# Order of work in one attention step, and fp16 parts of the attention output made on GpSimd

## The chip, the cores and the metric

The kernel runs on one NeuronCore of a Trainium2 chip. The metric is the device time of one execution in microseconds (us). Three runs of the kernel before gave a median of 3019.1 us (3017.41 to 3022.62).

## The reference

One transformer block on a [1, 2048, 576] fp32 input: LayerNorm, attention with 32 heads of 18 columns each, a residual; LayerNorm, a gated MLP of width 4608, a residual.

```python
qkv = (x @ wqkv).reshape(B, S, 3, 32, 18)            # q, k, v
scores = einsum("bhqd,bhkd->bhqk", q, k) * 18 ** -0.5
o = einsum("bhqk,bhkd->bhqd", softmax(scores), v)
h = x + o.reshape(B, S, 576) @ wo                    # x inside attention is layernorm(x)
out = h + (gelu(g @ w_gate) * (g @ w_up)) @ w_down   # g = layernorm(h)
```

## The kernel before

Matrices are held as fp16 pairs (a rounded part and the rest) so that fp16 products come out near fp32. The span has three stages: the q, k, v products (to about 230 us), attention (to about 1690 us), and the MLP.

**Attention** works on groups of four heads (`g`, 8 of them) and blocks of 512 queries (`qc`, 4 of them): 32 blocks, counted by `n`. One block takes 16 steps (`kt`), each with 128 keys. One step does three things for different blocks at once:

- **scores** (`scores_pair`, L453 to L463): for two heads at a time TensorE multiplies K by Q into a two-bank PSUM tile (`pair0`, `pair1` in turn), and ScalarE takes the exponential of both banks in one instruction (L463) into one of four buffers `pes`.
- **maxima** (`max_unit`, L408 to L425): softmax needs the row maximum beforehand, so the same products with queries on the partitions are computed once more, 28 units of 128 queries by 512 keys ahead. One call gives a pair: two matmuls (L420) into two banks of a ring of three (`m_ring`), each followed by a VectorE reduction over 512 columns (L423). A bank is written again three products later, after its reduction. `max_finish` (L427 to L446) folds a block's maxima: three small VectorE instructions (L430, L432, L433), then, a few steps later, a TensorE transpose into a ring bank (L438), a VectorE copy (L440) and eight small DMAs on SyncE's queue.
- **weighing** (`weigh`, L465 to L469): four matmuls (L467; eight records in the profile) add the previous step's exponentials times V into bank 3. It works one step behind the scores.

At a block's end `out_block` (L471) copies the sum to SBUF on ScalarE (L476), transposes it in a ring bank (four matmuls, L480), and on VectorE takes the reciprocal (L483) and multiplies (L485) into `o`, a [128, 4, 72] fp32 tile with two buffers. Then `o` is split into fp16 parts in `nat16`: a cast (L490) and one or two subtractions (L491, and L493 where the columns pass 512). In the last head group SyncE's transposing DMAs (L226) read these parts, and `wo_block` multiplies them by `wo` (as `fill`, a generator that is drawn between the scores, from step 4 of a block on).

**What sets the order.** TensorE's instructions are issued in the order in which the program is written (a manual schedule), by the loop over `n` and `kt` in the diff below. On VectorE, ScalarE and GpSimd a planner sets each queue's order at build time by its own estimates of when operands are ready; each queue is then strictly in order. GpSimd's queue also issues half of the loads of the next group's stacked q and k rows (L407, L408, 12 per group); SyncE's issues the other half.

Of the kernel before, what the change touches and what calls it, by code (L numbers as in the profile page):

```python
# [17 lines left out]
D = 576  # L18
H = 32
DH = 18  # L20
# [9 lines left out]
def tile_block(  # L30
# [17 lines left out]
    nc = tc.nc  # L48
# [4 lines left out]
    NT = S // P  # L53
# [161 lines left out]
    LM = D + TAIL  # L215
# [9 lines left out]
    def turn(rows, t):  # L225
        nc.sync.dma_start_transpose(XT[:, :, t * P : (t + 1) * P], rows)  # L226
# [42 lines left out]
    def run(it):  # L269
        for _ in it:  # L270
            pass
# [8 lines left out]
    def take(it, n=1):  # L280
        for _ in range(n):
            next(it, None)
# [105 lines left out]
    def init_set(st):  # L388
        for pr in range(2):
            for j in range(2):  # L390
                nc.sync.dma_start(
                    st[pr][1][64 * j + R1 : 64 * j + R1 + 2].rearrange("p (a b) -> p a b", b=256),
                    neg.unsqueeze(1).to_broadcast([2, S // 256, 256]))

    def load_stacks(g):
        st = sets[g % 2]
        for pr in range(2):
            eng = nc.sync if pr == 0 else nc.gpsimd
            Q, K = st[pr]
            for j in range(2):  # L400
                h = 4 * g + 2 * pr + j
                o = 64 * j
                kr = slice(D + h * DH, D + (h + 1) * DH)
                qr = slice(h * DH, (h + 1) * DH)
                for i, (qs, ks) in enumerate(((qk_hi, qk_hi), (qk_hi, qk_lo), (qk_lo, qk_hi))):
                    rows = slice(o + i * DH, o + (i + 1) * DH)
                    eng.dma_start(Q[rows], qs[qr])  # L407
                    eng.dma_start(K[rows], ks[kr])  # L408
# [45 lines left out]
    def scores_pair(n, kt, pr):  # L454

        g, qc = divmod(n, NB)
        pS = next(pair_ring)
        Q, K = sets[g % 2][pr]
        for j in range(2):
            r = half(j, R1 + 2)  # L460
            nc.tensor.matmul(pS[:, j, :TB], K[r, kt * P : (kt + 1) * P],  # L461
                             Q[r, qc * TB : (qc + 1) * TB], start=True, stop=True)
        nc.scalar.activation(pes[(2 * kt + pr) % NPE], pS[:, :, :TB], AF.Exp, scale=ex_sc)  # L463

    def weigh(n, kt, acc):  # L465
        for hh in range(4):
            nc.tensor.matmul(acc[32 * hh : 32 * hh + 32, :TB],  # L467
                             Vg[n // NB][:, kt * G4 + hh * VC : kt * G4 + hh * VC + 32],
                             pes[(2 * kt + hh // 2) % NPE][:, hh % 2],  # L469
                             start=(kt == 0), stop=(kt == NT - 1))  # L470

    def out_block(n, acc):

        g, qc = divmod(n, NB)
        oT = oTs[n % 2]
        nc.scalar.copy(oT, acc[:, :TB])  # L476
        yield
        pt = next(m_ring)
        for i in range(TPB):
            nc.tensor.transpose(pt[:, i * P : (i + 1) * P], oT[:, i * P : (i + 1) * P], id32)  # L480
        v = pt[:, :TB].rearrange("p (t h c) -> p t h c", h=4, c=32)
        rc = small.tile([P, TPB, 4, 1], F32, tag="rc", name="rc")
        nc.vector.reciprocal(rc, v[:, :, :, DH : DH + 1])  # L483
        o = small.tile([P, TPB, 4 * DH], F32, tag="o", name="o")
        nc.vector.tensor_mul(o.rearrange("p t (h c) -> p t h c", c=DH), v[:, :, :, :DH],  # L485
                             rc.to_broadcast([P, TPB, 4, DH]))
        f0 = g * 4 * DH
        f1 = min(f0 + 4 * DH, NK * P)
        dst = nat16[:, qc * TPB : (qc + 1) * TPB]
        nc.scalar.copy(dst[:, :, f0 : f0 + 4 * DH], o)  # L490
        nc.vector.tensor_sub(dst[:, :, LM + f0 : LM + f1], o[:, :, : f1 - f0], dst[:, :, f0:f1])  # L491
        if f1 < f0 + 4 * DH:
            nc.vector.tensor_sub(dst[:, :, D:LM], o[:, :, f1 - f0 :], dst[:, :, f1:D])  # L493

    NS = NG * NB
    UPS = TPB * NB
# [3 lines left out]
    def maxima():  # L500

        late = None
        for n in range(NS):
            mx = small.tile([P, TPB, 4, NB], F32, tag="mx", name="mx")
            for u in range(UPS):
                for i, _ in enumerate(max_unit(n, u, mx)):
                    yield
                    if late is not None and 2 * u + i == LAG:
                        for _ in late:
                            pass  # L510
                        late = None
            late = max_finish(n, mx)
            next(late)
        for _ in late:
            pass
# [22 lines left out]
    def wo_block(b):  # L538

        for t in range(b * TPB, (b + 1) * TPB):  # L540
            for i in range(2):
                ws = slice(i * HALF, (i + 1) * HALF)
                xb = xbs[(2 * t + i) % 3]
                nc.sync.dma_start(xb, xv[:, t, ws])
                pt = next(m_ring)
                run(accumulate(pt[:, :HALF], products(slice(t * P, (t + 1) * P), oh, ol, ws)))
                nc.vector.scalar_tensor_tensor(nat[:, t, ws], pt[:, :HALF], u_o, xb,
                                               op0=ALU.mult, op1=ALU.add)
                yield
            row_stats(nat[:, t], t)  # L550
        rstd_of(b * TPB, TPB)
        for t in range(b * TPB, (b + 1) * TPB):
            normed(y, nat[:, t], t)
            split_rows(ys[t % 2], y, nc.vector.tensor_copy if b < NB - 1 else nc.scalar.copy)
            turn(ys[t % 2], t)
            yield
# [84 lines left out]
    def qk_block(b):  # L641
        for j in (0, 4, 5):
            yield from qk_tile(j, b, next(m_ring))

    def v_block(b):
        for t in range(b * TPB, (b + 1) * TPB):
            yield from v_rows(t)

    def other_products():
        for b in range(1, NB):  # L650
            yield from v_block(b)
        for j in (1, 6, 2, 7, 3, 8):
            for b in range(NB):
                yield from qk_tile(j, b, next(pair_ring)[:, 0])
# [3 lines left out]
    def keep(it):  # L658
        kept.append((yield from it))

    mxs = maxima()
    with tc.manual_schedule(engines={EngineType.PE}):
        for b in range(NB):
            run(qk_block(b))
            if b == min(1, NB - 1):
                run(v_block(0))
        init_set(sets[0])
        load_stacks(0)
        fill = other_products()
        side = iter(())  # L670
        take(fill, 14)
        for i in range(2 * AHEAD):
            take(mxs)
            take(fill, 2 - i % 2)
        prev = None
        for n in range(NS):
            g, qc = divmod(n, NB)
            acc = singles[3]
            for kt in range(NT):
                for pr in range(2):  # L680
                    scores_pair(n, kt, pr)
                    take(mxs, UPS // NT)
                    if g < NG - 1 or kt >= NT // 4:
                        take(fill)
                    take(side)
                if prev is not None:
                    weigh(*prev)
                    if prev[0] != n:
                        ob = out_block(prev[0], prev[2])
                        next(ob)  # L690
                prev = (n, kt, acc)
                if n and kt == 1:
                    take(ob)
                    if n > NS - NB:
                        for t in range((qc - 1) * TPB, qc * TPB):
                            turn(nat16[:, t], t)
                        run(fill)
                        fill = wo_block(qc - 1)
                if g == 0 and qc == 0 and kt == NT - 1:
                    run(fill)  # L700
                    init_set(sets[1])
                if g + 1 < NG and kt == 2 and qc == (1 if g == 0 and NB > 1 else 0):
                    load_stacks(g + 1)
                if n == min(2, NS - 2) and kt == 2:
                    side = prepare_wo()
                if n == NS - NB and kt == 2:
                    load_gate_up(0)
                if n == max(NS - 2, NS - NB) and kt == NT * 3 // 4:
                    run(side)
                    side = keep(split_gate_up(0))  # L710
        weigh(*prev)
        for _ in out_block(prev[0], prev[2]):
            pass
        run(side)
        run(fill)
# [45 lines left out]
```

## Time and profile before

| | |
|---|---|
| median of 3 runs | 3019.1 us |
| the profiled execution's own time | 3017.52 us |
| its span | 3015.8 us |
| busy: TensorE / VectorE / ScalarE / GpSimd | 2792.8 / 1993.3 / 1454.6 / 62.9 us |
| granted TensorE clock, mean | 0.995 |
| maxima reductions (L423) | 2048, 1283.2 us busy |
| exponentials (L463) | 1024, 1088.0 us busy |
| casts of `o` on ScalarE (L490) | 32, 13.5 us busy |
| subtractions of `o` on VectorE (L491, L493) | 32 and 4, 13.3 and 1.7 us busy |

A row of a timeline gives the start in us from the span's beginning, the duration (from the first start to the last end where several instructions are merged, with their count behind an x), the engine, the source line, output and inputs; brackets hold the idle time ahead and what ended it. In the names, `pair` and `bank` are PSUM tiles, `A` and `W` are the two regions that hold the stacked q and k rows in turn, `WK` holds the exponentials.

### The profile page before, as it was taken

Reading aid. Unit: us, or ns where it says so; the run is one execution under the profiler, and the core shown is the slowest. Engines: PE = TensorE matmul, PEld = TensorE weight load, DVE = VectorE, ACT = ScalarE, POOL = GpSimd, SP = SyncE. Lnnn points to the kernel's source line nnn. Section 1 sums busy time; section 2 is a strip of 40 time slices with the busy share of each in tenths; the row PEclk is TensorE's granted clock in tenths of the full one; section 3 lists DMA queues with packets and bytes.
Section 4 is the critical chain, followed back from the end, with each engine's and each line's share of the span. In section 5 each row is a group of like instructions: output and inputs, shape, how many; then the busy total and the mean of one; then the engine's idle time right before and its main releaser. Section 6 shows DMA issues by size and latency. Waiting matters only on the chain.

```text
span 3015.8 us, 42951 instructions
## 1 busy us (share of the span) xinstructions
PE 2792.8 (93%) x17312; PEld 1154.9 (38%) x17312; DVE 1993.3 (66%) x3711; ACT 1454.6 (48%) x1716; POOL 62.9 (2%) x137
## 2 busy tenths in 40 slices
PE   6998888888888888888889999999999999999999
PEld 3531112212111211211123455555555555555555
DVE  7569999999999999999996653443435252524222
ACT  5227777777777777777757422121212121212111
POOL 0000000000000000000000000000000000000000
PEclk9999999999999999999999999999999999999999
DMA  8121000000100000000023420110101010100001
GB/s 222 49 87 32 1 25 1 25 1 1 25 1 25 1 24 2 1 24 5 29 48 87 100 67 7 45 33 19 51 1 52 1 51 1 51 1 1 1 16 48
DMA packets 105433, 95.14 MB, mean 32 GB/s; under 512 B 65872, under 2 KB 79312, under 8 KB 105232
## 3 DMA queue, kind: packets, MB, share of 16 engines
q1 hardware_dynamic: 100256, 83.81, 9.8%
q0 software_dynamic: 4976, 8.56, 1.1%
q8 instruction: 136, 2.23, 0.3%
q14 instruction: 65, 0.53, 0.1%
HBM read 63.70 MB, written 14.16 MB: 26 GB/s over the span
## 4 chain that ended last, share of the span: by engine, by line
PE 74%; DVE 18%; ACT 4%; issue 2%; DMA 2%; SPq 0%; DVEq 0%; ACTq 0%
PE pair L267 30%; PE bank L267 16%; DVE mx L423 15%; PE bank L467 14%; PE bank L420 9%; PE pair L461 4%; ACT WK L463 1%; ACT W L238 1%; ACT V L238 1%; PE bank L480 1%; DVE o L485 0%; ACT V L598 0%; DVE nat L491 0%; DMA A<-qk_hi 0%; DMA WK<-in_A_wqkv_dram 0%
## 5 line engine op out<-in xcount | busy, mean ns | idle before, releaser
L423 DVE TENSOR_REDUCE mx<-bank 128x1 f32<-128x512 f32 x2048 | 1283.2, 682 | 138.4 <-PE bank L420 137.4
L463 ACT ACTIVATE WK<-pair,p_ex_sc 128x1024 f32<-128x1024 f32 x1024 | 1088.0, 1112 | 335.1 <-PE pair L461 333.4
L467 PE MATMUL bank<-WK,V 128*32 128x512 f32 x4096 | 551.9, 610 | 0.1
L267 PE MATMUL pair<-X,V 128*128 128x512 f16 x2240 | 489.0, 379 | 3.1 <-ACT ga L613 3.1
L267 PE MATMUL pair<-X,W 128*128 128x512 f16 x2128 | 469.0, 379 | 1.5 <-ACT ga L613 1.5
L615 DVE SCALAR_TENSOR_TENSOR ga<-pair,p_hsc,ga 128x512 f32<-128x512 f32 x144 | 107.7, 748 | 502.4 <-PE pair L267 502.4
L420 PE MATMUL bank<-W 54*128 54x512 f16 x1024 | 291.5, 378 | 93.2 <-DVE mx L423 91.1
L267 PEld LDWEIGHTS <-WK 128*128 128x128 f16 x3456 | 338.2, 98 | 93.2
L420 PE MATMUL bank<-A 54*128 54x512 f16 x1024 | 283.0, 380 | 80.5 <-DVE mx L423 77.7
L613 ACT ACTIVATE ga<-pair,p_gsc 128x512 f32<-128x512 f32 x144 | 98.8, 686 | 490.2 <-PE pair L267 490.2
L267 PEld LDWEIGHTS <-W 128*128 128x128 f16 x2296 | 222.2, 98 | 273.1 <-issue 16.9
L267 PEld LDWEIGHTS <-V 128*128 128x128 f16 x2240 | 218.7, 98 | 261.6 <-issue 3.9
L616 ACT CAST WK<-ga 128x512 f16<-128x512 f32 x144 | 88.9, 618 | 442.9 <-DVE ga L615 442.9
L634 DVE SCALAR_TENSOR_TENSOR nat<-bank,p_dsc,nat 128x288 f32<-128x288 f32 x288 | 147.9, 515 | 194.9 <-PE bank L267 194.9
L467 PEld LDWEIGHTS bank<-WK,V 128*32 128x32 f32 x4096 | 81.3, 108 | 504.5 <-issue 469.0
L267 PE MATMUL bank<-V,WK 128*128 128x288 f16 x1920 | 239.0, 286 | 0.0
L461 PE MATMUL pair<-W 56*128 56x512 f16 x1024 | 199.1, 384 | 5.8 <-ACT WK L463 5.6
L461 PE MATMUL pair<-A 56*128 56x512 f16 x1024 | 199.9, 385 | 0.3 <-DVE qk L322 0.2
L267 PE MATMUL bank<-W,WK 128*128 128x288 f16 x1536 | 191.4, 286 | 0.0
L617 DVE TENSOR_TENSOR WK<-ga,WK 128x512 f16<-128x512 f32 x144 | 99.3, 690 | 76.3 <-ACT WK L616 76.1
L461 PEld LDWEIGHTS <-W 56*128 56x128 f16 x1024 | 50.2, 94 | 247.9 <-issue 221.0
L461 PEld LDWEIGHTS <-A 56*128 56x128 f16 x1024 | 50.5, 95 | 241.3 <-issue 211.0
(154 smaller groups left out, 1122.0 us busy)
## 6 DMA issues: line engine op xcount, KB each, us to landing
V<-in_B_w_down_dram SPq DMA_DIRECT2D x9, 1152.0 KB
A<-in_B_w_gate_dram SPq DMA_DIRECT2D x9, 1024.0 KB
A<-in_B_w_up_dram SPq DMA_DIRECT2D x9, 1024.0 KB
qk_hi<-qk SPq DMA_DIRECT2D x36, 128.0 KB
qk_lo<-qk SPq DMA_DIRECT2D x36, 128.0 KB
A<-in_A_x_dram SPq DMA_DIRECT2D x32, 144.0 KB
out_dram<-nat SPq DMA_DIRECT2D x16, 288.0 KB
WK<-in_A_wqkv_dram SPq DMA_DIRECT2D x3, 1152.0 KB
```

The costliest lines, as they stand in the source:

```text
L238: nc.scalar.activation(wh[:, c], wf[:, c], AF.Copy, scale=sc)
L267: nc.tensor.matmul(dst, a, b, start=(i == 0), stop=(i == len(pairs) - 1))
L420: nc.tensor.matmul(pms[j][:, :TB], Q[r, q0 : q0 + P], K[r, kc * TB : (kc + 1) * TB], start=True, stop=True)
L423: nc.vector.tensor_reduce(mx[:, t, 2 * pr + j, kc : kc + 1], pms[j][:, :TB], axis=AX.X, op=ALU.max)
L461: nc.tensor.matmul(pS[:, j, :TB], K[r, kt * P : (kt + 1) * P], Q[r, qc * TB : (qc + 1) * TB], start=True, stop=True)
L463: nc.scalar.activation(pes[(2 * kt + pr) % NPE], pS[:, :, :TB], AF.Exp, scale=ex_sc)
L467: nc.tensor.matmul(acc[32 * hh : 32 * hh + 32, :TB], Vg[n // NB][:, kt * G4 + hh * VC : kt * G4 + hh * VC + 32], pes[(2 * kt + hh // 2) % ...
L613: nc.scalar.activation(ga, pg[:, :TB], AF.Gelu_apprx_tanh, scale=gsc)
L615: nc.vector.scalar_tensor_tensor(ga, pu[:, :TB], hsc, ga, op0=ALU.mult, op1=ALU.mult)
L616: nc.scalar.copy(hh[:, f], ga)
L617: nc.vector.tensor_sub(hl[:, f], ga, hh[:, f])
L634: nc.vector.scalar_tensor_tensor(nat[:, t, ws], pt[:, :HALF], dsc, nat[:, t, ws], op0=ALU.mult, op1=ALU.add)
```

## The change

Two edits. In a step, both pairs of maxima used to follow the scores, one after each pair of heads (`take(mxs, UPS // NT)` takes one pair, since `UPS // NT` is 1). Now one pair stands ahead of the scores of all four heads and one behind them, ahead of the weighing. And the split of `o` (L490 to L493) moves to GpSimd: the cast from ScalarE, the subtractions from VectorE.

```diff
         dst = nat16[:, qc * TPB : (qc + 1) * TPB]
-        nc.scalar.copy(dst[:, :, f0 : f0 + 4 * DH], o)
-        nc.vector.tensor_sub(dst[:, :, LM + f0 : LM + f1], o[:, :, : f1 - f0], dst[:, :, f0:f1])
+        nc.gpsimd.tensor_copy(dst[:, :, f0 : f0 + 4 * DH], o)
+        nc.gpsimd.tensor_sub(dst[:, :, LM + f0 : LM + f1], o[:, :, : f1 - f0], dst[:, :, f0:f1])
         if f1 < f0 + 4 * DH:
-            nc.vector.tensor_sub(dst[:, :, D:LM], o[:, :, f1 - f0 :], dst[:, :, f1:D])
+            nc.gpsimd.tensor_sub(dst[:, :, D:LM], o[:, :, f1 - f0 :], dst[:, :, f1:D])
...
             for kt in range(NT):
+                take(mxs)
                 for pr in range(2):
                     scores_pair(n, kt, pr)
-                    take(mxs, UPS // NT)
                     if g < NG - 1 or kt >= NT // 4:
                         take(fill)
                     take(side)
+                take(mxs)
                 if prev is not None:
                     weigh(*prev)
```

On TensorE, in an ordinary step, from one weighing (L467) to the second scores of the next step. Banks 68 to 70 are the ring of the maxima, 66 and 67 the two score tiles, 71 the sum. Before:

```order
L467 MATMUL bank_71<-WK,V 32x512 x4
L461 LDWEIGHTS W
L461 MATMUL pair_66<-W 128x512 [waits Activation_49]
L461 LDWEIGHTS W
L461 MATMUL pair_66<-W 128x512
L420 LDWEIGHTS W
L420 MATMUL bank_69<-W 128x512 [waits DVE_49]
L420 LDWEIGHTS W
L420 MATMUL bank_70<-W 128x512 [waits DVE_49]
L461 LDWEIGHTS W
L461 MATMUL pair_67<-W 128x512 [waits Activation_49]
```

With the change:

```order
L467 MATMUL bank_71<-WK,V 32x512 x4
L420 LDWEIGHTS W
L420 MATMUL bank_69<-W 128x512 [waits DVE_49]
L420 LDWEIGHTS W
L420 MATMUL bank_70<-W 128x512 [waits DVE_49]
L461 LDWEIGHTS W
L461 MATMUL pair_66<-W 128x512 [waits Activation_49]
L461 LDWEIGHTS W
L461 MATMUL pair_66<-W 128x512
L461 LDWEIGHTS W
L461 MATMUL pair_67<-W 128x512 [waits Activation_49]
```

The first maxima now come straight behind the weighing, with two score matmuls fewer between; the two pairs of scores follow each other directly.

On VectorE, at a block's end, where the transposed sum stands in bank 70. Before:

```order
L423 TENSOR_REDUCE mx<-bank_69 128x1 [waits PE_49]
L483 RECIPROCAL rc<-bank_70 128x16 [waits PE_49]
L485 TENSOR_TENSOR o<-bank_70,rc 128x288 [waits DVE_49]
L423 TENSOR_REDUCE mx<-bank_68 128x1 [waits PE_49]
L423 TENSOR_REDUCE mx<-bank_69 128x1 [waits PE_49]
L491 TENSOR_TENSOR nat<-o,nat 128x4x72 [waits Activation_49]
L423 TENSOR_REDUCE mx<-bank_70 128x1 [waits PE_49]
```

With the change:

```order
L423 TENSOR_REDUCE mx<-bank_69 128x1 [waits PE_49]
L483 RECIPROCAL rc<-bank_70 128x16 [waits PE_49]
L423 TENSOR_REDUCE mx<-bank_68 128x1 [waits PE_49]
L485 TENSOR_TENSOR o<-bank_70,rc 128x288 [waits DVE_49,Pool_49]
L423 TENSOR_REDUCE mx<-bank_69 128x1 [waits PE_49]
L423 TENSOR_REDUCE mx<-bank_70 128x1 [waits PE_49]
```

The subtraction has left, one reduction has moved between the reciprocal and the product, and the product now waits for GpSimd, which reads the buffer of two blocks ago.

On GpSimd, where a new group's rows are loaded (`A` here), the queue with the change:

```order
L490 CAST nat<-o 128x4x72 [waits DVE_49]
L407 DMA A<-qk_hi 18x2048 [waits DMASW1_49,PE_49]
L491 TENSOR_TENSOR nat<-o,nat 128x4x72 [waits Pool_49]
L408 DMA A<-qk_hi 18x2048 [waits DMASW2_49]
L407 DMA A<-qk_hi 18x2048 [waits DMASW3_49]
```

Before, only the loads stood there; now the cast and the subtraction stand among them once per group, and alone in the queue for the other blocks.

## The prediction

> **What bounds the kernel now.** I read the page's chain first, then the long middle stage by windows, then the timeline of one step, then the steps that differ from it.
>
> ```profile
> PE 74%; DVE 18%; ACT 4%; issue 2%; DMA 2%; SPq 0%; DVEq 0%; ACTq 0%
> PE pair L267 30%; PE bank L267 16%; DVE mx L423 15%; PE bank L467 14%; PE bank L420 9%; PE pair L461 4%; ACT WK L463 1%; ACT W L238 1%; ACT V L238 1%; PE bank L480 1%; DVE o L485 0%; ACT V L598 0%; DVE nat L491 0%; DMA A<-qk_hi 0%; DMA WK<-in_A_wqkv_dram 0%
> ```
>
> The attention part of the chain is not one engine's: reductions (L423), weighing (L467), maxima products (L420) and, with 4%, scores (L461) alternate. So no engine is full there, and the windows say the same:
>
> ```profile
> 502.25:1523.00 1020.75, 890.97 (x5989) 201.96 (x5987) 944.04 (x1640) 796.28 (x780) 30.65 (x62) 1.00 0.05 12
> ```
>
> In order: length, busy TensorE, weight loads, VectorE (944 of 1021 us, 92%), ScalarE, GpSimd, clock 1.00. One ordinary step shows what closes the loop:
>
> ```profile
> 802.25 0.39 PE L461 MATMUL pair<-W 56*128 56x512 f16 x2
> ...
> 802.48 0.38 PE L420 MATMUL bank<-W 54*128 54x512 f16 x2
> ...
> 802.70 0.38 PE L461 MATMUL pair<-W 56*128 56x512 f16 x2
> ...
> 802.74 2.12 ACT L463 ACTIVATE WK<-pair,p_ex_sc 128x1024 f32<-128x1024 f32 x2 [0.57 <-PE pair L461]
> 802.89 2.48 DVE L423 TENSOR_REDUCE mx<-bank 128x1 f32<-128x512 f32 x4 [0.21 <-PE bank L420]
> ...
> 803.64 0.37 PE L420 MATMUL bank<-W 54*128 54x512 f16 x1 [0.34 <-DVE mx L423]
> ...
> 803.94 1.07 PE L467 MATMUL bank<-WK,V 128*32 128x512 f32 x8
> ...
> 804.94 0.39 PE L461 MATMUL pair<-W 56*128 56x512 f16 x2
> ...
> 805.16 0.38 PE L420 MATMUL bank<-W 54*128 54x512 f16 x2
> ...
> 805.58 2.48 DVE L423 TENSOR_REDUCE mx<-bank 128x1 f32<-128x512 f32 x4 [0.20 <-PE bank L420]
> ```
>
> The step's first reduction starts at 802.89. The fourth maxima product writes the same bank, and starts 0.75 later (803.64). The weighing follows 0.30 after it, TensorE's next matmul 1.00 after that (804.94, the scores), the next first maximum 0.22 behind those (805.16), and its reduction 0.42 later (805.58). 0.75 + 0.30 + 1.00 + 0.22 + 0.42 = 2.69 us, the whole period: each link is on the loop. VectorE's four reductions take 2.48, and stand 0.20 idle. A reduction lasts 0.68 but the next starts 0.60 after it ((2.48 - 0.68) / 3), so VectorE alone could do a step in 4 x 0.60 = 2.40.
>
> **The order inside the step.** The scores' 0.22 leaves the loop, since the first maxima now stand straight behind the weighing. What the head of the queue costs is seen only for scores: from 802.25 to the exponential at 802.74 is 0.49, against 0.42 from a maxima product to its reduction. Part of that 0.07 is ScalarE's answer and part the second matmul it needs; so 0.42 to 0.49 are the ends, and I take 0.43, nearest to the row of the same two engines. The step becomes 0.75 + 0.30 + 1.00 + 0.43 = 2.48 us, 0.21 less, and VectorE's idle time falls from 0.20 to 0.08.
>
> Three other waits must stay covered; let the first maximum start at 0. *Banks:* the second product of the next step writes the bank of the third reduction, which starts 1.20 after the first, lasts 0.68, and is answered 0.07 later (0.75 - 0.68): 1.95 after the first reduction; TensorE comes out of the weighing at 0.75 + 0.30 + 1.00 = 2.05. Cover 0.10. *Exponentials:* the scores start at 0.22, the exponentials 0.49 later at 0.71, and end at 2.83, which is 0.35 into the next step; the second scores, due at 0.44 there, need the tile of the second one. Cover 0.09; and behind them the second maxima wait until 0.43 + 0.75 = 1.18 anyway, though they could go at 0.66, so another 0.52 stands behind it. *Weighing* uses exponentials of the step before, ready at 0.35, and starts at 1.48.
>
> **A block of 16 steps.** The sum's copy (L476) marks blocks:
>
> ```profile
> 502.25 0.58 ACT L476 COPY WK<-bank 128x512 f32<-128x512 f32 x1 [0.18 <-PE bank L467]
> 546.62 0.58 ACT L476 COPY WK<-bank 128x512 f32<-128x512 f32 x1 [0.18 <-PE bank L467]
> ...
> 1525.73 0.58 ACT L476 COPY WK<-bank 128x512 f32<-128x512 f32 x1 [0.18 <-PE bank L467]
> ...
> L476 ACT COPY WK<-bank x32: 585/585/595, 275.1 to 1685.9; 128x512 f32<-128x512 f32 x32
> ```
>
> One block is 44.37 us; from 275.1 to 1525.73 there are 28. Sixteen steps are 43.04; three steps are longer.
>
> *Transposing the maxima.*
>
> ```profile
> 827.86 1.29 DVE L423 TENSOR_REDUCE mx<-bank 128x1 f32<-128x512 f32 x2 [0.20 <-PE bank L420]
> ...
> 828.60 0.37 PE L420 MATMUL bank<-W 54*128 54x512 f16 x1 [0.40 <-DVE mx L423]
> ...
> 829.06 0.20 DVE L440 COPY mT<-bank 32x128 f16<-32x128 f16 x1
> ...
> 829.20 0.37 PE L420 MATMUL bank<-W 54*128 54x512 f16 x1 [0.23 <-DVE mx L423]
> ...
> 831.14 2.48 DVE L423 TENSOR_REDUCE mx<-bank 128x1 f32<-128x512 f32 x4 [0.68 <-PE bank L420]
> ```
>
> The transpose takes a ring bank, so the step's last product waits for the second reduction instead of the first: 831.14 - 827.86 = 3.28, or 0.59 over. The transpose still stands ahead of the second maxima pair and still takes their bank: 0.59 stays.
>
> *Folding the maxima* puts three small instructions between reductions:
>
> ```profile
> 822.48 0.69 DVE L423 TENSOR_REDUCE mx<-bank 128x1 f32<-128x512 f32 x1 [0.20 <-PE bank L420]
> ...
> 823.21 0.68 DVE L423 TENSOR_REDUCE mx<-bank 128x1 f32<-128x512 f32 x1
> ...
> 823.89 0.68 DVE L423 TENSOR_REDUCE mx<-bank 128x1 f32<-128x512 f32 x1
> ...
> 824.57 3.08 DVE L423 TENSOR_REDUCE mx<-bank 128x1 f32<-128x512 f32 x5
> ```
>
> Starts are 0.73, 0.68, 0.68 apart, not 0.60: 0.29 more, which idle time hid (the next first reduction at 824.57 + 0.60 = 825.17, so the step stayed 2.69). Now VectorE needs 2.40 + 0.29 = 2.69 against 2.48: 0.21 over.
>
> *The block's output:*
>
> ```profile
> 858.01 2.48 DVE L423 TENSOR_REDUCE mx<-bank 128x1 f32<-128x512 f32 x4 [0.21 <-PE bank L420]
> ...
> 860.06 0.66 PE L480 MATMUL bank<-id,WK 128*128 128x128 f32 x4
> ...
> 860.64 0.10 PEld L461 LDWEIGHTS <-W 56*128 56x128 f16 x2 [0.17 <-issue]
> ...
> 860.75 0.26 DVE L483 RECIPROCAL rc<-bank 128x16 f32<-128x16 f32 x1 [0.26 <-PE bank L480]
> ...
> 861.04 0.46 DVE L485 TENSOR_TENSOR o<-bank,rc 128x288 f32<-128x288 f32 x1
> ...
> 861.42 1.28 DVE L423 TENSOR_REDUCE mx<-bank 128x1 f32<-128x512 f32 x2
> ...
> 862.98 3.67 DVE L423 TENSOR_REDUCE mx<-bank 128x1 f32<-128x512 f32 x6
> ```
>
> Before: the first reduction comes 3.41 after the last one (861.42 - 858.01), 0.72 over; the third starts at 862.98 instead of 862.62, since the subtraction takes 0.36, and the next first one at 862.98 + 2 x 0.60 = 864.18, 2.76 later, 0.07 over. Together 0.79. So the subtraction cost 0.07 of its 0.36; most of it lay in VectorE's idle time.
> Now: the transposes push the first maxima back by 0.58 (860.06 to 860.64). The reciprocal is done by then (transposes + 0.69 + 0.29 = 0.98, reduction at 0.58 + 0.43 = 1.01). The third and fourth products write the bank out of which `o` is made, so they wait for one reduction and then the product, 0.38 longer (861.04 to 861.42). Together 0.96. Without the second edit the subtraction's 0.36 would come on top where VectorE has 0.08 left, some 0.3 per block, 9 us in all: that is what the move to GpSimd is worth. The cast on ScalarE cost nothing that ends last.
>
> New block: 16 x 2.48 + 0.59 + 0.21 + 0.96 = 41.44; the same sum for before, 43.04 + 0.59 + 0.79 = 44.42, is close to the 44.37 seen. Saved: 44.37 - 41.44 = 2.93; 28 blocks: 82 us.
>
> **Outside these blocks.** 484 steps hold maxima (1024 pairs less 56 taken ahead, two a step); 448 are counted. Of the other 36 about half run with other products drawn in, where TensorE is full; the rest gives 18 x 0.21 = 4 us (466 steps in all). Against it, 20 VectorE instructions of preparing `wo` (five maxima, five splits) and the first gate and up weights (ten maxima) lay partly in the idle time, which shrinks by 0.12 a step: 20 x 0.12 = 2.5 us lost.
>
> **The cost on GpSimd.** No row shows arithmetic like it. Nearest:
>
> ```profile
> masks.py:199 POOL TENSOR_SCALAR_AFFINE_SELECT id<-id 128x128 f32<-128x128 f32 x1 | 0.3, 282 | 0.0
> ```
>
> 0.282 us for 128 columns, so at most 0.63 for the cast's 288 and, with two inputs, 1.27 for the subtraction, 1.9 in all; at least what the two engines take now. `o` has two buffers, so a block (41 us) covers this 20 times, also behind twelve loads. It shows only where a transposing DMA waits for it:
>
> ```profile
> 1688.04 0.43 ACT L490 CAST nat<-o 128x288 f16<-128x288 f32 x1 [1.59 <-DVE o L485]
> ...
> 1688.61 0.42 DVE L493 TENSOR_TENSOR nat<-o,nat 128x256 f16<-128x256 f32 x1
> ...
> 1689.10 6.01 SPq L226 DMA_TRANSPOSE X<-nat  x4
> ```
>
> Now 1.06 from cast to DMA; with GpSimd 1.06 to 1.9. At most twice on the path (here and one block earlier): 0 to 1.7, I take 1.0 in all.
> The Trainium skill (GPSIMD Engine Reference, section 3.1) gives about 2.6 cycles per element at 1.2 GHz for two inputs, by which the subtraction would be an estimated 0.62 us and the tail's loss smaller; no run here shows it yet.
>
> **Sum:** 82 + 4 - 2.5 - 1 = 82 us. From the profiled execution's 3017.5: 2935. The median of the runs lies 1.6 above that execution: 2937 us.
>
> **Rivals.**
> *Half the gain.* The first maxima pay at the head of the queue what the scores paid there, 0.49, and one of the thin covers (0.09, 0.10) is missed by some hundredths: step 2.59, gain 0.10 x 466 - 4 = 43 us, 2976. For it: covers this thin. Against: missing the exponentials' cover has 0.52 behind it.
> *VectorE becomes the bound.* If the links behind the weighing are shorter without scores, the step is 2.40: another 0.08 x 466 = 37, less what folding then costs anew (0.08 x 28): 2902. For: VectorE is 92% busy. Against: 0.30 and 1.00 are TensorE's own.
> *GpSimd holds VectorE.* If VectorE stands while GpSimd reads `o`, each block loses up to 1.9 us: 32 x 1.9 = 61, 2998.
>
> ```profile
> L423 DVE TENSOR_REDUCE mx<-bank x2048: 661/680/693, 95.7 to 1598.2; 128x1 f32<-128x512 f32 x187
> ```
>
> Against: no reduction is stretched (least, median, greatest ns) though GpSimd issues loads among them; but none of its instructions there reads SBUF. The Trainium skill (SBUF — State Buffer, Who interferes with whom) says that a GpSimd read and a VectorE instruction with two SBUF inputs exclude each other, and that reductions never contend on this chip; by that rule the reductions go on, and only the small folding instructions could be held, eight reductions later.
> *Slower.* Both score pairs now need their tiles within 0.22. If the two exponentials end D later than the 2.12 shown, the second scores hold everything behind them in TensorE's queue: second maxima, weighing, next step. From D = 0.61 the step grows one for one; from 0.82 it is longer than before. At D = 1.0 it is 2.87: 0.18 x 466 = 84 us slower, 3103. For: cover 0.09. Against: no step shows such an exponential.
> *Nothing changes.* VectorE's and ScalarE's queues follow a planner; where a late instruction sits in VectorE's queue, each block could lose the gain again: 3019. Against: their order at a block's end follows the new arrivals.
>
> **How the numbers follow.** Forecast 0.71; half 0.12; VectorE bound 0.07; GpSimd holds 0.03; slower 0.04; nothing 0.03. The forecast's own ends: 0.49 at the head (0.06 x 466 = 28, 2965) and a step 0.05 shorter (2914). Range 2908 to 2972, which leaves out the outer rivals and part of the half gain. This kernel tells 0.2% (6 us) from no change: faster 0.71 + 0.12 + 0.07 + 0.03 = 0.93, same 0.03, slower 0.04.
>
> **What would show it.** An ordinary step of 2.48 with VectorE's idle time 0.08 and the fourth product still waiting for a reduction; blocks of 41.4 by L476; the transposing step still 0.59 over. Wrong if the second scores wait for L463, if L423 lasts over 0.69, or if steps stay above 2.6.

## The result: 2926.8 us instead of 3019.9

The changed kernel takes 2926.81 us (2924.51 to 2927.78, four runs), the kernel before on the same chip 3019.87 us (3017.41 to 3022.62, four runs): the ratio is 0.9691, interval 0.9674 to 0.9707. The forecast was 2937 us, so the change gave 93 us where 82 were forecast. The profiled span fell from 3015.8 to 2922.7 us.

**The stage.** The page's row of the maxima reductions and a window of 960 us in the attention stage, changed kernel:

```profile
L423 DVE TENSOR_REDUCE mx<-bank 128x1 f32<-128x512 f32 x2048 | 1282.2, 683 | 61.4 <-PE bank L420 58.8
```

```profile
473.00:1433.00 960.00, 889.38 (x6065) 214.78 (x6060) 942.74 (x1629) 795.97 (x767) 57.16 (x108) 1.00 0.04 13
```

VectorE is now busy for 942.74 of 960 us, 98% where it was 92%. The reductions cost what they did (683 ns each); the idle time ahead of them fell to 61.4 us (138.4 on the page of before). The granted clock is 1.00 in this window in both kernels, so the gain is not the clock's. The chain of waits helps no further: its shares add up to about half the span, so what follows is read from the timeline.

**An ordinary step** of the changed kernel:

```profile
796.47 7.49 DVE L423 TENSOR_REDUCE mx<-bank 128x1 f32<-128x512 f32 x12
...
796.91 1.07 PE L467 MATMUL bank<-WK,V 128*32 128x512 f32 x8
...
797.91 0.39 PE L420 MATMUL bank<-W 54*128 54x512 f16 x2
...
798.13 0.60 PE L461 MATMUL pair<-W 56*128 56x512 f16 x4
...
798.57 0.88 PE L420 MATMUL bank<-W 54*128 54x512 f16 x2
798.62 2.12 ACT L463 ACTIVATE WK<-pair,p_ex_sc 128x1024 f32<-128x1024 f32 x2 [0.35 <-PE pair L461]
...
799.38 1.07 PE L467 MATMUL bank<-WK,V 128*32 128x512 f32 x8
```

From weighing to weighing it is 799.38 - 796.91 = 2.47 us (2.69 before). The first maxima stand straight behind the weighing, 1.00 after its start; the scores follow 0.22 later, in time that nothing waits for. Twelve reductions take 7.49, so one starts every (7.49 - 0.68) / 11 = 0.62 on average, where 0.60 is the closest that they come: under 0.1 of a step is left on VectorE. The two exponentials still take 2.12 and wait 0.35 for scores; no scores wait for them.

**The blocks**, by the copy of the sum:

```profile
270.46 0.58 ACT L476 COPY WK<-bank 128x512 f32<-128x512 f32 x1
...
771.70 0.58 ACT L476 COPY WK<-bank 128x512 f32<-128x512 f32 x1
...
813.00 0.58 ACT L476 COPY WK<-bank 128x512 f32<-128x512 f32 x1
...
1433.59 0.58 ACT L476 COPY WK<-bank 128x512 f32<-128x512 f32 x1
...
1592.68 0.59 ACT L476 COPY WK<-bank 128x512 f32<-128x512 f32 x1 [1.15 <-PE bank L467]
```

A block is 813.00 - 771.70 = 41.30 us (44.37 before). The first copy comes 4.6 us sooner than before (275.1), the one 28 blocks later 92.1 sooner (1525.73), the last 93.2 sooner (1685.9). So 87.5 us of the gain lie in these 28 blocks, and nearly all of it in attention.

**The three longer steps**, on VectorE and TensorE of the changed kernel, one block from its output on:

```profile
773.90 0.66 PE L480 MATMUL bank<-id,WK 128*128 128x128 f32 x4
774.59 0.26 DVE L483 RECIPROCAL rc<-bank 128x16 f32<-128x16 f32 x1 [0.25 <-PE bank L480]
774.91 0.69 DVE L423 TENSOR_REDUCE mx<-bank 128x1 f32<-128x512 f32 x1
775.52 0.45 DVE L485 TENSOR_TENSOR o<-bank,rc 128x288 f32<-128x288 f32 x1
775.88 5.04 DVE L423 TENSOR_REDUCE mx<-bank 128x1 f32<-128x512 f32 x8
776.02 0.39 PE L420 MATMUL bank<-W 54*128 54x512 f16 x2 [0.71 <-DVE o L485]
```

The transposes (773.90) push the first maxima to 774.49, and the last two products of the step wait for `o` (776.02). Weighings in this block start at 772.90, 776.34, 778.81, 781.28, 783.96, 787.03 and 789.50: the output step takes 3.44 (0.97 over 2.47), the folding step 2.68 (0.21 over), the transposing step 3.07 (0.60 over), all others 2.47. 16 x 2.47 + 0.97 + 0.21 + 0.60 = 41.30.

**GpSimd**, groups by line in the changed kernel (count | busy us, mean ns | idle before):

```profile
L491 POOL TENSOR_TENSOR nat<-o,nat 128x288 f16<-128x288 f32 x28 | 20.6, 736 | 1.8
L490 POOL CAST nat<-o 128x288 f16<-128x288 f32 x32 | 13.5, 423 | 1046.4 <-DVE o L485 1046.4
```

The cast takes 0.423 us, as it did on ScalarE (13.5 us for 32), the subtraction 0.736 where VectorE took 0.45 (its row in the order alone, below): 1.16 together, against the 1.9 set as the upper bound. The estimate of 0.62 us for the subtraction, worked out from the Trainium skill (GPSIMD Engine Reference, section 3.1), was nearer to the trace's 0.74 than the bound from the row of the mask (1.27).

### The profile page after: what moved, and what is told of

It is laid out like the page before. It is cut to its first block, busy times and chain, and to the rows that moved or that the text cites. A ratio compares the mean times of both kernels' runs of the same rounds, so it can differ in the third digit from the quotient of the medians.

```text
span 2922.7 us, 42983 instructions
## 1 busy us (share of the span) xinstructions
PE 2772.1 (95%) x17312; PEld 1168.1 (40%) x17312; DVE 1977.2 (68%) x3675; ACT 1440.0 (49%) x1684; POOL 100.4 (3%) x205
## 4 chain that ended last, share of the span: by engine, by line
PE 44%; ACT 3%; DVE 2%; DMA 1%; issue 1%; POOL 0%; ACTq 0%; SPq 0%
PE pair L267 27%; PE bank L267 15%; ACT WK L463 1%; DVE mx L423 1%; ACT W L238 1%; ACT V L238 1%; PE bank L467 1%; ACT V L598 0%; DMA X<-nat 0%; PE pair L461 0%; ACT W L598 0%; DMA X<-V 0%; DMA V<-in_B_w_down_dram 0%; ACT ga L613 0%; PE bank L420 0%
## 5 line engine op out<-in xcount | busy, mean ns | idle before, releaser
L423 DVE TENSOR_REDUCE mx<-bank 128x1 f32<-128x512 f32 x2048 | 1282.2, 683 | 61.4 <-PE bank L420 58.8
L467 PE MATMUL bank<-WK,V 128*32 128x512 f32 x4096 | 548.7, 607 | 0.1
L267 PEld LDWEIGHTS <-WK 128*128 128x128 f16 x3456 | 338.2, 98 | 93.2
L467 PEld LDWEIGHTS bank<-WK,V 128*32 128x32 f32 x4096 | 81.2, 108 | 409.2 <-issue 380.5
L461 PE MATMUL pair<-W 56*128 56x512 f16 x1024 | 161.1, 378 | 5.6 <-ACT WK L463 5.4
L420 PEld LDWEIGHTS <-W 54*128 54x128 f16 x1024 | 61.6, 93 | 242.2 <-issue 235.2
L461 PE MATMUL pair<-A 56*128 56x512 f16 x1024 | 157.1, 379 | 1.1 <-ACT WK L463 1.1
L420 PEld LDWEIGHTS <-A 54*128 54x128 f16 x1024 | 60.3, 93 | 231.4 <-issue 225.1
```

The costliest lines, as they stand in the source:

```text
L267: nc.tensor.matmul(dst, a, b, start=(i == 0), stop=(i == len(pairs) - 1))
L420: nc.tensor.matmul(pms[j][:, :TB], Q[r, q0 : q0 + P], K[r, kc * TB : (kc + 1) * TB], start=True, stop=True)
L423: nc.vector.tensor_reduce(mx[:, t, 2 * pr + j, kc : kc + 1], pms[j][:, :TB], axis=AX.X, op=ALU.max)
L467: nc.tensor.matmul(acc[32 * hh : 32 * hh + 32, :TB], Vg[n // NB][:, kt * G4 + hh * VC : kt * G4 + hh * VC + 32], pes[(2 * kt + hh // 2) % ...
```

## The experiments

Two theories at first: the scores' 0.22 us on the loop explain the gain (then the order alone carries it, and any place on the loop costs it); or VectorE's and ScalarE's relief by GpSimd does. Later runs ask what holds the step at 2.47.

**The order alone.** L490 to L493 go back to ScalarE and VectorE.

```diff
-        nc.gpsimd.tensor_copy(dst[:, :, f0 : f0 + 4 * DH], o)
-        nc.gpsimd.tensor_sub(dst[:, :, LM + f0 : LM + f1], o[:, :, : f1 - f0], dst[:, :, f0:f1])
+        nc.scalar.copy(dst[:, :, f0 : f0 + 4 * DH], o)
+        nc.vector.tensor_sub(dst[:, :, LM + f0 : LM + f1], o[:, :, : f1 - f0], dst[:, :, f0:f1])
         if f1 < f0 + 4 * DH:
-            nc.gpsimd.tensor_sub(dst[:, :, D:LM], o[:, :, f1 - f0 :], dst[:, :, f1:D])
+            nc.vector.tensor_sub(dst[:, :, D:LM], o[:, :, f1 - f0 :], dst[:, :, f1:D])
```

> The new order of the step alone; the fp16 parts of o stay on ScalarE and VectorE. Theory (the loop reduction, fourth product, weighing, first product got shorter by the scores' 0.22): the ordinary step stays 2.47; the subtraction's 0.36 lies between reductions in the output step, where VectorE has 0.07 to 0.08 left, so a block is 41.30 + 0.28 = 41.6 us and the time 2927 + 31 x 0.28 = 2935 us (2931 to 2940). Rival (the move to GpSimd carries the gain, by relieving ScalarE and VectorE): blocks near 44 and 2990 us or more.

Measured: 2933.07 us, ratio 0.9722 (0.9707 to 0.9736) to 3016.23 on that chip. Its timeline:

```profile
817.50 0.58 ACT L476 COPY WK<-bank 128x512 f32<-128x512 f32 x1
859.07 0.58 ACT L476 COPY WK<-bank 128x512 f32<-128x512 f32 x1
...
864.44 0.45 DVE L491 TENSOR_TENSOR nat<-o,nat 128x288 f16<-128x288 f32 x1
864.81 0.68 DVE L423 TENSOR_REDUCE mx<-bank 128x1 f32<-128x512 f32 x1
```

A block is 41.57. The subtraction holds the next reduction for 0.37 (864.44 to 864.81), of which 0.27 per block show, 7.5 us in 28 blocks. The order carries the rest.

**The move to GpSimd alone**, in the old order:

```diff
             for kt in range(NT):
-                take(mxs)
                 for pr in range(2):
                     scores_pair(n, kt, pr)
+                    take(mxs, UPS // NT)
...
-                take(mxs)
                 if prev is not None:
```

> The move of the fp16 parts to GpSimd alone, in the old order. Theory: the step stays 2.69 and only the 0.07 that the subtraction put on the path goes: block 44.30 us, time 3020 - 2 = 3018 us, not to be told from before. Rival (the move carries the gain): 2950 us or less.

Measured: 3015.77 us, ratio 0.9998 (0.9989 to 1.0007). Its timeline:

```profile
765.91 0.58 ACT L476 COPY WK<-bank 128x512 f32<-128x512 f32 x1 [0.19 <-PE bank L467]
810.29 0.58 ACT L476 COPY WK<-bank 128x512 f32<-128x512 f32 x1 [0.18 <-PE bank L467]
```

44.38 per block, as before: not even the 0.07 that were expected. In the old order `o` starts 0.36 us after the reciprocal with the move and 0.29 without it. In 27 of the 32 blocks L485 now has a wait for GpSimd's semaphore ahead of it; the five blocks without that wait keep 0.29. That took back the 0.07. So the move is worth 7 us behind the new order and nothing by itself: the two edits are no sum of two gains.

**Maxima first, but one pair before each pair of scores:**

```diff
             for kt in range(NT):
-                take(mxs)
                 for pr in range(2):
+                    take(mxs)
                     scores_pair(n, kt, pr)
...
-                take(mxs)
                 if prev is not None:
```

> The change, but with the second pair of scores behind the second pair of maxima: maxima, scores, maxima, scores, weighing. The first maxima still stand straight behind the weighing. Theory (one score pair on the loop costs its 0.22 wherever it stands between the product that waits for the reduction and the next first product): step 0.75 + 0.22 + 0.30 + 1.00 + 0.42 = 2.69, block 16 x 2.69 + 0.60 + 0.96 = 44.6 us, time 2927 + 28 x 3.3 = 3019 us (3010 to 3030). Rival (what counts is that maxima stand first behind the weighing, so that VectorE is fed early): 2.47 and 2927 us.

Measured: 3025.05 us, ratio 1.0025 (1.0015 to 1.0035), blocks of 44.57. Its timeline:

```profile
799.31 0.38 PE L420 MATMUL bank<-W 54*128 54x512 f16 x1
...
800.03 0.37 PE L420 MATMUL bank<-W 54*128 54x512 f16 x1 [0.35 <-DVE mx L423]
800.04 0.59 PE L461 MATMUL pair<-W 56*128 56x512 f16 x2
800.55 1.07 PE L467 MATMUL bank<-WK,V 128*32 128x512 f32 x8
```

The second scores now stand between the fourth product (800.03) and the weighing, 0.52 apart instead of 0.30. The whole gain is gone, though the first maxima stand ahead of all scores. What matters is not which comes first, but that no scores lie between the fourth product and the next first one.

**The output later in the step**, behind the scores and ahead of the second maxima (the block below moves up over `take(mxs)` and the weighing):

```diff
+                if n and kt == 1:
+                    take(ob)
...
                 take(mxs)
                 if prev is not None:
                     weigh(*prev)
...
-                if n and kt == 1:
-                    take(ob)
...
```

> The change, with the four transposes of a block's output moved from behind the weighing of step 1 to ahead of the second maxima of step 1 (behind the scores). Theory (the loop by its links): the transposes no longer push the first maxima back by 0.58, nor does the third product wait for o (0.38); instead the ring is one bank short in that step, so the fourth product waits for the second reduction, 0.60. The step is 0.60 over instead of 0.97; block 40.93 us, time 2927 - 31 x 0.37 = 2915 us (2911 to 2921). Rival (VectorE is the bound now, its work is the same): 2927 us.

Measured: 2915.31 us, ratio 0.9664 (0.965 to 0.9679). Its timeline:

```profile
766.87 0.59 ACT L476 COPY WK<-bank 128x512 f32<-128x512 f32 x1
...
768.22 0.25 DVE L483 RECIPROCAL rc<-bank 128x16 f32<-128x16 f32 x1
...
807.77 0.59 ACT L476 COPY WK<-bank 128x512 f32<-128x512 f32 x1
```

40.90 per block, 0.40 less. The transposes no longer stand between the weighing and the first maxima, and no idle time stands ahead of the reciprocal any more (0.25 in the changed kernel). This supports the prediction's reading of the output step (0.58 of transposes ahead of the first maxima).

**GpSimd's work on `o` done six times:**

```diff
-        nc.gpsimd.tensor_copy(dst[:, :, f0 : f0 + 4 * DH], o)
-        nc.gpsimd.tensor_sub(dst[:, :, LM + f0 : LM + f1], o[:, :, : f1 - f0], dst[:, :, f0:f1])
+        for _ in range(6 if g < NG - 1 else 1):
+            nc.gpsimd.tensor_copy(dst[:, :, f0 : f0 + 4 * DH], o)
+            nc.gpsimd.tensor_sub(dst[:, :, LM + f0 : LM + f1], o[:, :, : f1 - f0], dst[:, :, f0:f1])
```

> The change, with the cast and the subtraction of o on GpSimd done six times over in the first seven head groups (same result, about 7 us of GpSimd work a block instead of 1.2, so that it also runs while VectorE folds the maxima). Theory (GpSimd's work is covered by o's second buffer, and it holds up nothing on VectorE): 2927 us, blocks 41.30, L432 and L433 at 0.16 us as before. Rival (the rule that a VectorE instruction with two SBUF inputs, or a small copy-like one, waits for a GpSimd instruction that reads SBUF): L432 and L433 stretched by up to 0.7 us each, blocks up to 1 us longer, 2935 to 2955 us, while the reductions L423 stay at 0.68.

Measured: 2929.23 us, ratio 0.9709 (0.9696 to 0.9723), against 0.9691 with once. Most blocks are 41.37 to 41.39, each fourth, where the group loads lie, 41.71 to 42.00. The total is near the theory's; that folding instructions are held is the rival's. Timeline of this kernel, and its view of the folded maxima (least, median, greatest ns):

```profile
781.89 0.73 POOL L492 TENSOR_TENSOR nat<-o,nat 128x288 f16<-128x288 f32 x1
782.41 0.25 DVE L433 SCALAR_TENSOR_TENSOR mm<-m,mm 128x16 f16<-128x16 f32 x1
782.58 3.74 DVE L423 TENSOR_REDUCE mx<-bank 128x1 f32<-128x512 f32 x6
```

```profile
L433 DVE SCALAR_TENSOR_TENSOR mm<-m,mm x32: 158/249/377, 161.4 to 1507.8; 128x16 f16<-128x16 f32 x32
```

L433, with two inputs in SBUF, ends only once GpSimd's subtraction has (782.62): 0.249 instead of 0.163 in the middle. In six of the blocks with the group loads L432, with one input, is held as well (0.37 to 0.66 instead of 0.16), and L433 takes 0.37: what the two lose, 0.42 to 0.70, is what these blocks are longer than 41.30. The reductions, which read PSUM, keep 627/681/694 ns. So GpSimd can hold VectorE, as the Trainium skill says (SBUF — State Buffer, Who interferes with whom), for the instructions it names, and the trace agrees on the reductions too. But five extra turns cost 0.08 in three blocks of four and 0.4 to 0.7 in the fourth, and the change's single turn, over long before the folding (776.03 to 777.26 against 780.84), nothing: L433 kept its 0.163 there.

**The folding's two small instructions on GpSimd** (L432 and L433 as three):

```diff
-        nc.vector.tensor_scalar_mul(mm[:, :, 0], m, 1 / MSC)
-        nc.vector.scalar_tensor_tensor(mm[:, :, 1], m, 1 / MSC, mm[:, :, 0],
-                                       op0=ALU.mult, op1=ALU.subtract)
+        nc.gpsimd.tensor_scalar_mul(m, m, 1 / MSC)
+        nc.gpsimd.tensor_copy(mm[:, :, 0], m)
+        nc.gpsimd.tensor_sub(mm[:, :, 1], m, mm[:, :, 0])
```

> The change, with two of the three small folding instructions (L432, L433) moved from VectorE to GpSimd (as a scaling, a cast and a subtraction). Theory (VectorE has 0.07 us left in a step, so of the folding's 0.29 the step shows 0.21): folding costs VectorE 0.13, the step is 0.06 over instead of 0.21, block 41.15, time 2927 - 31 x 0.15 = 2922 us (2920 to 2925). Rival (the folding is hidden): blocks 41.30, 2927 us.

Measured: 2920.88 us, ratio 0.9683 (0.967 to 0.9696); blocks of 41.13, 0.17 less. The intervals of this ratio and the change's overlap, so the blocks decide. Most of the folding step's 0.21 was VectorE's, as the prediction said, and did not lie on the loop before.

**Both**, the later output and the folding on GpSimd:

> The change with both the late output transposes and the folding on GpSimd. Theory (the two act in different steps and add): block 40.92 - 0.15 = 40.77, time 2915 - 5 = 2910 us. Rival (one takes the other's idle time): 2915 us.

Measured: 2910.72 us (2910.51 to 2912.42), ratio 0.9649 (0.9636 to 0.9662); blocks of 40.76. Of the versions that leave nothing out this is the fastest, some 13 us ahead of the changed kernel by the two ratios (0.9649 and 0.9691, each to the kernel before on its own chip).

**One of four heads weighed** (the other three are left out):

```diff
-        for hh in range(4):
+        for hh in range(1):
...
+    nc.vector.memset(singles[3], 1.0)
```

> The change, but only the first of a group's four heads is weighed (three of the four matmuls L467 are left out, the other rows hold ones), which makes the weighing shorter and nothing else. Theory (the loop through the weighing is 2.47, VectorE alone 2.40): the loop drops below VectorE's own work, the ordinary step becomes 2.40, the folding shows its 0.29 whole, the transposing step 0.13 over, the output step 0.67; block 16 x 2.40 + 1.09 = 39.5 us, time 2927 - 31 x 1.8 = 2871 us (2865 to 2885). Rival (VectorE is the bound already at 2.47): 41.30 and 2927 us.

Measured, in one run: 2912.89 us (3017.53 before). From its timeline:

```profile
799.38 1.04 PE L467 MATMUL bank<-WK,V 128*32 128x512 f32 x2
800.36 0.39 PE L420 MATMUL bank<-W 54*128 54x512 f16 x2
```

The experiment did not do what it was meant to: one head's weighing holds TensorE for 0.98 us where four hold it for 1.00, so the four, on 32 columns of the array each, run at once. The loop lost 0.02, and the block 0.31 (40.99): 16 x 0.02. It tells that a change of 0.02 on the loop shows in full, not what holds the step once the loop is well below 2.47.

**Weighing in only 4 of 16 steps** (the rest is left out):

```diff
-                    weigh(*prev)
+                    if prev[1] % 5 == 0:
+                        weigh(*prev)
```

> The change, but only every fifth step's exponentials are weighed (steps 0, 5, 10, 15; the other twelve weighings of a block are left out, so the loop through the weighing is open in twelve steps of sixteen). Theory (the step is the longer of the loop, 2.47, and VectorE's four reductions, 2.39 to 2.40): VectorE runs without a gap; 64 reductions, folding 0.29, copy 0.13, output 0.67 make 39.5 us a block and the four steps with weighing at most 0.3 more, 39.5 to 39.8; time 2927 - 31 x 1.65 = 2876 us (2868 to 2884). Rival (without the weighing another wait, for exponentials or banks, keeps 2.47): 41.0 and 2920 us; or VectorE was not near its bound: far below 2868.

Measured, in one run: 3021.0 us, a miss of 145 us. With three quarters of the weighing gone it is slower than the change by 94. From its timeline:

```profile
883.20 1.93 PE L467 MATMUL bank<-WK,V 128*32 128x512 f32 x8
...
885.67 8.46 DVE L423 TENSOR_REDUCE mx<-bank 128x1 f32<-128x512 f32 x14 [1.11 <-PE bank L420]
```

and windows of 3.41 us of the same stretch (length, busy TensorE with its matmuls; the granted clock is the third number from the end):

```profile
875.22:878.63 3.41, 2.51 (x11) 0.67 (x10) 3.41 (x7) 3.14 (x4) 0.00 (x0) 1.00 0.00 0
878.63:882.05 3.42, 3.18 (x12) 0.70 (x11) 3.42 (x7) 2.73 (x3) 0.00 (x0) 0.50 0.00 0
882.05:885.46 3.41, 3.41 (x15) 0.46 (x15) 2.32 (x4) 2.25 (x3) 0.00 (x0) 0.50 0.02 5
885.46:888.88 3.42, 2.75 (x16) 0.74 (x13) 3.21 (x6) 2.70 (x3) 0.00 (x0) 1.00 0.00 0
```

Steps without weighing ran at VectorE's pace, (8.46 - 0.68) / 13 = 0.60 per reduction, 2.39 a step, as the theory had it. But the granted clock fell to 0.50 for whole windows of 3.41 us (0.71 on average from 473 to 1520 us), and each weighing in such a window took 1.93 instead of 1.07, with VectorE idle for 1.11 behind it. Blocks are 44.19 and 44.55 in turn. So the expectation failed on something it had not asked: whether the clock stays.

**Two banks in the maxima's ring instead of three:**

```diff
-    m_ring = ring(singles[:3])
+    m_ring = ring(singles[:2])
```

> The change with a ring of two banks for the maxima instead of three. Theory (the loop runs through the reduction whose bank the product ahead of the weighing writes): the fourth product waits for the second reduction instead of the first, 0.60 later, step 2.47 + 0.60 = 3.07; the output step about 1.5 over, since the second maximum then waits for o; block 16 x 3.07 + 0.1 + 1.5 = 50.7 us, time 2927 + 30 x 9.4 = 3210 us (3195 to 3235). Rival (banks do not set the step, VectorE does): 2927 to 2940 us.

Measured, in one run: 3241.33 us. From its timeline, and windows of 3.41 us around an output step:

```profile
736.73 1.07 PE L467 MATMUL bank<-WK,V 128*32 128x512 f32 x8
...
739.80 1.07 PE L467 MATMUL bank<-WK,V 128*32 128x512 f32 x8
```

```profile
719.59:723.00 3.41, 1.93 (x12) 0.76 (x12) 2.26 (x5) 0.67 (x1) 1.15 (x2) 1.00 0.00 0
723.00:726.41 3.41, 3.41 (x16) 0.66 (x16) 1.71 (x4) 1.73 (x3) 0.00 (x0) 0.50 0.00 0
726.41:729.82 3.41, 2.84 (x19) 0.62 (x17) 2.83 (x6) 2.67 (x3) 0.00 (x0) 1.00 0.00 0
```

The step is 3.07 and the block 50.84: 0.60, one reduction, more on the loop, as expected from "the fourth product waits for a reduction in the same bank". The total is above the expected: the first copy comes 31.6 us later (302.05 against 270.46), and about each third block is 1.1 to 1.3 longer, where the window after the output's stall ran at half clock.

**Half of the columns weighed** (256 of 512 queries; the other half of `o` is left out). It shortens the weighing itself, which the run with one head did not:

```diff
-            nc.tensor.matmul(acc[32 * hh : 32 * hh + 32, :TB],
+            nc.tensor.matmul(acc[32 * hh : 32 * hh + 32, : TB // 2],
...
-                             pes[(2 * kt + hh // 2) % NPE][:, hh % 2],
+                             pes[(2 * kt + hh // 2) % NPE][:, hh % 2, : TB // 2],
...
+    nc.vector.memset(singles[3], 1.0)
```

> The weighing of each step takes only the first 256 of the 512 query columns (the other half of o is left out, so the output differs); order, banks, maxima, scores and exponentials stay as in the changed kernel. A weighing takes 0.98 to 1.00 us on the loop of the changed kernel's step of 2.47 us; on half the columns it should take some 0.5 us, and the loop would then close in about 2.0 us, below VectorE's four reductions, which the kernel with 12 of 16 weighings left out ran at 8.46 us for 14, 0.604 each, 2.42 a step. Theory A (the weighing is on the loop, and VectorE's 2.40 to 2.42 is the floor below it; TensorE keeps its granted clock of 1.00): an ordinary step 2.42, a block 41.30 - 16 x 0.05 = 40.5 (VectorE is busy for 40.52 us of a block of 41.30), the whole 2927 - 32 x 0.8 = 2901 (2895 to 2910). Theory B (the granted clock falls to about a half in part of the blocks when TensorE has less work, as it did with 12 weighings left out, where a step with a weighing then took 3.7 us): a step at half clock 3.7 - 0.95 = 2.75, a block between 41 and 46, the whole 2930 to 3070, with a clock under 0.9 in the attention stage. Theory C (the weighing is not on the loop): a block of 41.30, 2927.

Measured, in one run: 2869.28 us (3014.52 before), with a clock of 1.00 from 473 to 1429 us. From its timeline:

```profile
808.27 0.64 PE L467 MATMUL bank<-WK,V 128*32 128x256 f32 x8
808.84 0.70 PE L420 MATMUL bank<-A 54*128 54x512 f16 x2
...
810.66 0.64 PE L467 MATMUL bank<-WK,V 128*32 128x256 f32 x8
```

A weighing holds TensorE for 0.57 and the step is 2.39: the weighing was on the loop, and VectorE is the floor below it. The size was off: blocks are 39.41, not 40.5. I had taken VectorE's busy time in a block, 40.52, for its floor; but a reduction's row lasts 0.68 where the next can start 0.60 after it, so a gap of up to 0.08 between two of them does not show as idle, and busy time takes it for work. The weighings' spacing gives the floor right: 16 x 2.39 + 0.62 (output) + 0.29 (folding) + 0.25 (transposing, over two steps) = 39.40.

## Why the prediction was right, point by point

- **The scores' 0.22 leaves the loop: right.** Step 2.47, 2.48 forecast. The order alone, the one with scores back on the loop, and half the weighing each moved the step as this loop says.
- **Head of the queue, taken at 0.43 (0.42 to 0.49): 0.42.** In the changed kernel the step of 2.47 leaves 0.42 beside 0.75 + 0.30 + 1.00. The first maxima pay nothing of what the scores paid. This 0.01 is 0.14 per block with the rest of the sum, 3.9 us in 28 blocks.
- **Transposing step, 0.59 over: 0.60. Folding, 0.21 over: 0.21. Output step, 0.96 over: 0.97.** All from rows of before, all within 0.01.
- **The block, 41.44: 41.30. Saved in 28 blocks, 82: 87.5.** 28 x 3.07 are 86.0; the other 1.5 come from the few blocks that hold preparation of weights, chiefly from one that got 4.80 shorter.
- **20 instructions of preparation cost 2.5: wrong in sign.** These blocks gained 1.5 instead. What failed is that the same instructions stay in these blocks: the block that got 4.80 shorter held eight of the reductions L122 before (5.33 us on VectorE) and holds three now (2.01 us); the other five stand in the next block, outside the 28. Idle time that shrinks does show: in the one block with a single such reduction in both kernels, it made the block 0.29 longer than the others before (44.67 against 44.38) and 0.51 now (41.81 against 41.30), so 0.22 more where 0.12 was forecast. That the planner's move outweighs this is luck.
- **Outside the 28 blocks, 4 us: 5.7.** 4.6 ahead of the first copy (2.6 to 5.5 in the five experiments with this order, three banks and the whole weighing) and 1.1 behind the 28 blocks (93.2 - 92.1).
- **The tail, 1.0 lost: about nothing.** The bounds held, the middle was too high. The last block of the changed kernel:

```profile
1594.89 0.42 POOL L490 CAST nat<-o 128x288 f16<-128x288 f32 x1 [44.18 <-DVE o L485]
...
1595.60 0.67 POOL L493 TENSOR_TENSOR nat<-o,nat 128x256 f16<-128x256 f32 x1
1596.29 4.68 SPq L226 DMA_TRANSPOSE X<-nat  x3
```

  From cast to DMA 1.40 instead of 1.06; but the last copy is 93.2 us earlier than before and the span 93.1 shorter, so at most 0.1 was lost behind it.
- **The covers held.** From 473 to 1433 us no score waited for an exponential, and in the rows shown no product waited for a bank but the one counted on. Of the thin covers (0.09, 0.10) none was used up, so "half the gain" and "slower" did not come about.
- **The move to GpSimd hides a cost of 9 us: about 7.** 0.27 per block where 0.3 was forecast.
- **VectorE as the bound: not yet.** It idles 0.08 per step. The price that the prediction put on it, 2902, was too high for what a shorter loop could reach: with half of the weighing left out, 2869, since then the output and the transposing step lose their stalls too, which the rival kept.

The miss of 11 us in all: 3.9 from the head, 4.0 from the preparation, 1.7 outside, about 1 from the tail.

## What to carry to other kernels

Where no engine is full, write down the loop that closes a step, link by link from the starts in a timeline, and look for work that stands between two links without being one: moving it into a link that waits anyway gains its whole time, and putting it back at another place of the loop loses it all. An engine's floor is the spacing of its back-to-back instructions, not its busy time. Relief of an engine is worth nothing while the loop has slack there, and shows only once the loop is as short as the engine.

## What the runs showed that was not expected

**Less work on TensorE can make it slower.** In the kernel with 4 weighings the clock went from 1.00 to 0.50 and back, for whole windows of 3.41 us: it fell at 861.57, rose at 871.81, fell at 878.63, rose at 885.46, fell at 888.88 and rose at 899.12, which is 3, 2, 2, 1 and 3 times 3.41. Single windows at 0.50 stand in other kernels too (341.99 to 345.40 in the changed one). In the windows shown above, those at full clock with 11, 16 and (with two banks) 12 matmuls are each followed by one at half clock. The Trainium skill (TensorE: Matmul & The Clock Gate, What's actually happening) gives a free-running window of 4096 cycles at 1.2 GHz, 3.413 us, and the trace agrees. It has the clock fall after an idle window; here TensorE was never idle for a window, but busy for 1.93 to 2.75 of 3.41 us in those before a fall, so the measurement decides: a window with gaps can be enough. How full it must be stays open, and neither the matmuls nor the busy time alone settle it: the kernel with half the weighing lost the clock behind a window of 23 matmuls, busy for 2.67 us (309.77 to 313.18), and the one with one head kept it behind one of 14, busy for 1.88 (1493.40 to 1496.81). The kernel with half the weighing has 1.00 from 473 to 1429 us, but 0.94 from 230 to 470 and 0.90 from 1429 to 1600, where the changed kernel has 0.99. So a shorter loop need not cost the clock in the ordinary blocks; less work on TensorE may cost it elsewhere.

**Four heads cost TensorE what one costs**, 1.00 against 0.98 us, when each uses 32 of its columns: the weighing's price on the loop is the 512 query columns, not the heads.

**One more semaphore to wait for costs 0.07 us** ahead of L485 (0.36 instead of 0.29 from the reciprocal's start, in the old order with the move to GpSimd). In the new order, with a reduction between the two, it costs nothing: 0.93 in the changed kernel (774.59 to 775.52), which has the wait, and 0.93 with the order alone, which has not.
